# Half rows of the w2 gradient stored from ScalarE's DMA queue in place of GpSimd's

## The chip, the cores and the metric

The kernel runs on one core of a Trainium2 chip. The metric is the device time of one execution in microseconds (us). A core has TensorE (PE in the profile, its weight loads PEld), VectorE (DVE), ScalarE (ACT), GpSimd (POOL) and SyncE (SP); the last issues transfers only. Each engine takes its instructions in the order in which the built program holds them. Transfers between the chip's DRAM and SBUF are issued by SyncE and GpSimd here, and, in the changed kernel, by ScalarE as well.

## The reference, cut to what matters

The reference is a block of two halves and its gradients: a spectral mixing layer (a 2-D FFT, a product with complex weights w_r + i w_i, the inverse FFT) and an MLP, each behind a layer norm with adaptive scale and shift from a conditioning vector.

```python
def _B_ref(x, w1, b1, w2, b2):            # S=2048, D=1024, F=3584
    y = _layernorm(x, axis=-1)
    h = _gelu(jnp.einsum('bsd,df->bsf', y, w1) + b1)
    return jnp.einsum('bsf,fd->bsd', h, w2) + b2
mod = (_silu(c) @ w_mod).reshape(c.shape[0], 6, 1, -1)      # sa, ca, ga, sb, cb, gb
h = _layernorm(x, axis=-1) * (1 + ca) + sa
x = x + ga * _A_ref(h, A_w_r, A_w_i)      # spectral half
h = _layernorm(x, axis=-1) * (1 + cb) + sb
x = x + gb * _B_ref(h, B_w1, B_b1, B_w2, B_b2)
_out, _vjp = jax.vjp(_f, A_x, A_w_r, A_w_i, B_w1, B_b1, B_w2, B_b2, c, w_mod)
return (_out0, *_vjp(grad_out))
```

All inputs and outputs are bfloat16. The output that the change touches is the gradient of w2 (out_6, 3584 x 1024): h transposed times gb * grad_out, a sum over the 2048 tokens.

## The kernel before, in words

The work is a sequence of stages, all written for one core. Forward: modulation rows, spectral half, MLP. Backward: first the MLP's gradient towards its input (pg_pass, by four token blocks), then the backward spectral half (spectral_core with fwd False). The gradients of w2 and w1 are large matrix products that wait for nobody; they are cut into pieces (the generator `pieces`, L1226) and handed to TensorE between the steps of the backward spectral half, as filling (`fill`, L1277).

**The w2 gradient.** It has 28 blocks `fc` of 128 rows, each in two halves `h` of 512 columns. One half (gw2_product, L1088) is 16 matmuls of 128 x 128 x 512 (gw2_mm, L1075) into one of four PSUM buffers (`ps_f`, "gw2acc"), each with a transposed slice of the hidden activations as its weights. These slices, 128 x 2048 of d_hh, come by transposing loads from SyncE (hh_load, L1228) into a few buffers, two blocks ahead. gw2_out (L1078) copies the PSUM buffer to SBUF (L1082), on whatever engine `nc.any` picks when the program is built: a scheduler with a model of each engine's time places every instruction and breaks ties by it. For fc below 8 the rows go to five buffers and are stored whole (L1086). From fc 8 on, two rows `gwo` of two halves serve by turns, and each half is stored by itself (L1084) from GpSimd's queue: 40 stores of 128 x 512 elements, 128 KB each. A copy into a half must wait until the store that last read this half has landed.

**The backward spectral half** around it, by line:

- Eight pairs n = 0 to 7 (`pair`, L495). A pair is 16 matmuls on TensorE (pcs, L505), four copies on ScalarE (cs01b, L650), then a chain on VectorE (L173): Pt from cs01b, products with the weights ws (qa, qb), the sums R, and the gradient of the spectral weights in pf or empf. SyncE stores that gradient (L551) and loads the next values of pf and of ws (L493, L490); GpSimd does the mirrored rows with indirect transfers (L552, L491). Four halves of the w2 gradient are filled in behind each pair (beside_bwd, L1302).
- In between, single steps of another gradient, that of w_mod (gmod_ring, L981): SyncE loads a piece of w_mod into one of three buffers in otl (L986, 256 KB, and L989 for a new row), VectorE reduces it (L997) and writes the outer product (L999), GpSimd stores it (L1000).
- s_inv (L556) turns R into V: per quarter eight products "pv" (L565) of four matmuls, each emptied by a copy (L647, also by `nc.any`), on two PSUM buffers. Two quarters follow the sixth pair, two the eighth.
- Then four groups of "po" products (L630) whose copies go to VectorE and ScalarE (L635, L637), and the chain of consume_bwd (L1184) on VectorE. The rest of the w2 gradient, and then the w1 gradient (gw1acc, L1266, stored by L1271 from GpSimd's queue), fills TensorE until the end. Its operands are the loads n3n (L1251) and, transposed, gzh (L1217).

**Semaphores.** Every transfer reports its landing to a semaphore. The framework gives the transfers of the hardware queues (SyncE's, and ScalarE's where there are any) eight of them by turns, and the software queue of GpSimd eight others; a transfer is issued only when the one that used its semaphore before has landed.

Of the kernel before, what the change touches and what calls it, by code (L numbers as in the profile page):

```python
# [17 lines left out]
P = 128  # L18
# [17 lines left out]
def kernel(  # L36
# [24 lines left out]
    nc = tc.nc  # L61
# [870 lines left out]
    for g in range(7):  # L932
        wtile = reg.tile([P, 4, D], BF16, name=f"w1T_{g}", tag=W1T[g])
        for k in range(4):
            fc = g * 4 + k
# [142 lines left out]
    def gw2_out(acc, fc, h):  # L1078
        row = gwo5[fc % 5] if fc < 8 else gwo[:, fc % 2]
        half = slice(h * KH, (h + 1) * KH)  # L1080
        with tc.high_priority():
            nc.any.tensor_copy(out=row[:, half], in_=acc[:])  # L1082
        if fc >= 8:
            nc.gpsimd.dma_start(out=out_6[fc * P:(fc + 1) * P, half], in_=row[:, half])  # L1084
        elif h == 1:
            nc.gpsimd.dma_start(out=out_6[fc * P:(fc + 1) * P, :], in_=row)  # L1086

    def gw2_product(fc, h):  # L1088
        acc = ps_f("gw2acc")
        for t in range(NT):  # L1090
            gw2_mm(acc, fc, h, t)
        gw2_out(acc, fc, h)
# [133 lines left out]
    def pieces():  # L1226
# [18 lines left out]
        for fc, h, acc in last:  # L1245
            gw2_out(acc, fc, h)
# [120 lines left out]
```

## Time and profile before

| what | us |
|---|---|
| median of three runs (lowest, highest) | 1463.76 (1459.10, 1466.73) |
| the profiled execution: time | 1459.13 |
| its span, first to last instruction | 1457.3 |
| TensorE busy (6835 matmuls) | 1396.5 |
| VectorE busy | 1058.4 |
| ScalarE busy | 752.2 |
| GpSimd busy | 366.1 |
| the 40 stores of L1084 on GpSimd, first and last start | 1057.5, 1239.3 |
| one such issue on GpSimd, median | 0.552 |
| one copy of L1082 on ScalarE, median | 0.585 |
| TensorE busy in the 205 us from 1040 to 1245 | 198.52 |

Times inside an execution count from the span's first instruction. "A <- B" in a view of waits reads: A stood idle until B had ended. A line "start, us, engine, line, operation, tiles, xcount [idle before <- releaser]" is one of a timeline. The granted TensorE clock of the profiled execution was 0.992 of full speed on average. The difference of 1.8 us between time and span lies outside the first and last instruction.

### The profile page before, as it was taken

How to read it: one execution, taken by the hardware profiler on the slowest of the kernel's cores; microseconds unless marked ns; L12 is line 12 of the kernel's file. 1: busy time of each engine (PE TensorE's matmuls, PEld its weight loads, DVE VectorE, ACT ScalarE, POOL GpSimd, SP SyncE). 2: the span in 40 equal slices, each digit the busy share in tenths (PEclk: the TensorE clock that was granted, in tenths of full speed). 3: DMA queues.
4: the chain of work that ended last, by engine and by line, in shares of the span. 5: the costliest groups of instructions: out<-in, count | busy, mean ns of one | idle time of the engine just before them, and what ended most of it. 6: DMA issues, size and time to landing. Idle time of an engine off the chain costs nothing. (4 is left out here: it accounts for less than half of the span.)

```text
span 1457.3 us, 18411 instructions
## 1 busy us (share of the span) xinstructions
PE 1396.5 (96%) x6835; PEld 649.0 (45%) x6835; DVE 1058.4 (73%) x1483; ACT 752.2 (52%) x1065; POOL 366.1 (25%) x441
## 2 busy tenths in 40 slices
PE   5889999999999999999999999999999999999997
PEld 2434545444444444444444444344444445444443
DVE  5884786898799787887520889898467678898650
ACT  4675555857887766665305574342622434344211
POOL 6520451211112122122211011021245441222432
PEclk8999999999999999999999999999999999999999
DMA  9962473899887877697998275297699987766991
GB/s 333 286 214 70 142 235 115 270 255 337 257 203 278 259 250 233 201 264 241 277 297 245 74 271 185 107 270 176 181 217 254 254 233 213 194 191 180 297 279 65
DMA packets 358367, 324.28 MB, mean 223 GB/s; under 512 B 209386, under 2 KB 301056, under 8 KB 358022
## 3 DMA queue, kind: packets, MB, share of 16 engines
q1 hardware_dynamic: 324166, 207.71, 52.7%
q0 software_dynamic: 34112, 115.41, 22.6%
q8 instruction: 53, 0.87, 0.2%
q14 instruction: 36, 0.29, 0.1%
HBM read 162.06 MB, written 111.20 MB: 188 GB/s over the span
## 5 line engine op out<-in xcount | busy, mean ns | idle before, releaser
L684 PE MATMUL pp<-gBoT,wt 128*128 128x512 bf16 x896 | 197.9, 380 | 4.5 <-DMA wt<-in_B_w_dram 2.6
L950 PE MATMUL pg<-w1T,gzr 128*128 128x512 bf16 x896 | 197.1, 381 | 0.2 <-ACT gn3b L961 0.2
L1266 PE MATMUL gw1acc<-gzh,n3n 128*128 128x512 bf16 x896 | 195.4, 379 | 1.3 <-DMA gzh<-d_gz 1.3
L684 PEld LDWEIGHTS <-wt 128*128 128x128 bf16 x896 | 87.7, 98 | 109.4 <-issue 4.2
L950 PEld LDWEIGHTS <-gzr 128*128 128x128 bf16 x896 | 87.3, 98 | 108.7 <-issue 6.6
L802 PEld LDWEIGHTS <-w 128*128 128x128 bf16 x896 | 87.3, 98 | 108.8 <-issue 4.7
L1266 PEld LDWEIGHTS <-n3n 128*128 128x128 bf16 x896 | 87.4, 98 | 106.1 <-issue 2.7
L802 PE MATMUL pz<-n3Tb,w 128*128 128x512 bf16 x448 | 99.2, 379 | 1.6 <-DVE w2sD L875 1.4
L802 PE MATMUL pz<-n3Ta,w 128*128 128x512 bf16 x448 | 98.7, 379 | 1.1 <-ACT gt L805 1.1
L1075 PE MATMUL gw2acc<-gB,hhsA 128*128 128x512 bf16 x448 | 98.5, 379 | 1.0 <-DMA hhsA<-d_hh 1.0
L853 PEld LDWEIGHTS <-hhA 128*128 128x128 bf16 x608 | 59.0, 98 | 71.7 <-issue 1.4
L805 ACT ACTIVATE gt<-pz,b_col 128x512 bf16<-128x512 f32 x112 | 72.5, 684 | 34.2 <-PE pz L802 32.8
L1270 ACT CAST gwo<-gw1acc 128x512 bf16<-128x512 f32 x50 | 29.1, 583 | 113.6 <-PE gw1acc L1266 99.0
L173 DVE TENSOR_TENSOR gt<-gt,gt 128x2048 bf16<-128x2048 bf16 x56 | 68.3, 1223 | 22.4 <-ACT gt L813 21.2
L1082 ACT CAST gwo<-gw2acc 128x512 bf16<-128x512 f32 x46 | 26.7, 583 | 109.9 <-PE gw2acc L1075 75.6
L811 ACT ACTIVATE gt<-gt 128x2048 bf16<-128x2048 bf16 x28 | 53.5, 1910 | 55.7 <-DVE gt L173 55.7
L173 DVE TENSOR_TENSOR ct<-ct 128x2048 bf16<-128x2048 bf16 x64 | 75.9, 1218 | 1.8 <-DMA d_n<-ct 1.1
L1075 PEld LDWEIGHTS <-hhsA 128*128 128x128 bf16 x448 | 43.6, 98 | 53.0 <-DMA hhsA<-d_hh 1.7
L997 DVE CUSTOM_DVE_ANT_0 otl<-otl 128x1024 bf16<-128x1024 bf16 x24 | 29.1, 1223 | 49.9 <-DMA otl<-in_w_mod_dram 44.2
L807 ACT ACTIVATE gt<-gt 128x2048 bf16<-128x2048 bf16 x28 | 53.4, 1908 | 5.4 <-DVE hhC L173 2.5
L813 ACT ACTIVATE gt<-gt 128x2048 bf16<-128x2048 bf16 x28 | 53.5, 1909 | 0.5
L1271 POOL DMA_DIRECT2D out_dram<-gwo x56 | 30.6, 548 | 85.6 <-ACT gwo L1270 53.4
(325 smaller groups left out, 2531.5 us busy)
## 6 DMA issues: line engine op xcount, KB each, us to landing
gzr<-d_gz SPq DMA_DIRECT2D x28, 512.0 KB
wblk<-in_w_mod_dram SPq DMA_DIRECT2D x12, 1024.0 KB
out_dram<-otl POOLq DMA_DIRECT2D x48, 256.0 KB
out_dram<-gwo POOLq DMA_DIRECT2D x96, 128.0 KB
d_ph<-pho POOLq DMA_DIRECT2D x21, 512.0 KB
d_hh<-hhA POOLq DMA_DIRECT2D x19, 512.0 KB
w2sD<-in_B_w_dram SPq DMA_DIRECT2D x14, 512.0 KB
hhC<-d_ph SPq DMA_DIRECT2D x14, 512.0 KB
```

Of the source, the lines that this page charges most:

```text
L173: return nc.vector.tensor_tensor(out=out, in0=a, in1=b, op=op)
L684: last_pe[0] = nc.tensor.matmul(pp[:], lhsT=wt[:, fg % 2, cch, k * P:(k + 1) * P], rhs=gBoT[j][:, cch, :], start=(cch == 0), stop=(cch == ...
L802: last_pe[0] = nc.tensor.matmul(pz[:], lhsT=w1s[g][:, cch, k * P:(k + 1) * P], rhs=n3T[:, cch, :], start=(cch == 0), stop=(cch == NDC - 1))
L805: nc.scalar.activation(out=zb[:, k, :], in_=pz[:], func=ACT.Identity, bias=b1_col[:, fc:fc + 1], scale=1.0)
L807: nc.scalar.activation(out=av, in_=zb, func=ACT.Square)
L811: nc.scalar.activation(out=sg, in_=bv, func=ACT.Sigmoid, scale=2.0 * GK)
L813: nc.scalar.activation(out=bv, in_=bv, func=ACT.Sigmoid, scale=-2.0 * GK)
L853: last_pe[0] = nc.tensor.matmul(pbs[i][:], lhsT=hh[:, k, i * P:(i + 1) * P], rhs=wp[:, k, :], start=False, stop=(g == 6 and k == 3))
L950: last_pg[0] = nc.tensor.matmul(pgs[i][:], lhsT=gzs[b, g][:, k, i * P:(i + 1) * P], rhs=w1Ts[g][:, k, h * KH:(h + 1) * KH], start=(g == 0 ...
L1075: nc.tensor.matmul(acc[:], lhsT=hh_of(fc)[:, t, :], rhs=gBs[t // 4][:, t % 4, h * KH:(h + 1) * KH], start=(t == 0), stop=(t == NT - 1))
L1266: nc.tensor.matmul(acc[:], lhsT=n3ns[t // 4][:, t % 4, cch * P:(cch + 1) * P], rhs=gz2[t // 8][:, t % 8, :], start=(t == 0), stop=(t == NT ...
L1271: nc.gpsimd.dma_start(out=out_4[cch * P:(cch + 1) * P, fg * 512:(fg + 1) * 512], in_=ob)
```

## The change

For fc of 8 and more, the copy out of PSUM is bound to ScalarE (it was `nc.any`), and the store of the half row is issued from ScalarE's own queue, inside the same block of high priority, in place of GpSimd's. For fc below 8 nothing changes.

```diff
         with tc.high_priority():
-            nc.any.tensor_copy(out=row[:, half], in_=acc[:])
-        if fc >= 8:
-            nc.gpsimd.dma_start(out=out_6[fc * P:(fc + 1) * P, half], in_=row[:, half])
-        elif h == 1:
+            (nc.any.tensor_copy if fc < 8 else nc.scalar.copy)(out=row[:, half], in_=acc[:])
+            if fc >= 8:
+                nc.scalar.dma_start(out=out_6[fc * P:(fc + 1) * P, half], in_=row[:, half])
+        if fc < 8 and h == 1:
             nc.gpsimd.dma_start(out=out_6[fc * P:(fc + 1) * P, :], in_=row)
```

In the built program the 40 stores leave GpSimd's order and stand in ScalarE's, each behind the copy that it stores; in six places the four pcs copies of a pair stand between the two, and among the last four stores another copy of L1082. SyncE's instructions keep their order. The two copies of L1082 that VectorE had are ScalarE's now. Since the scheduler places the rest by its model, some other instructions move as well, none of them before the first of these stores: two copies of L647 from ScalarE to VectorE, and the order of po, gw1acc and of VectorE's chain in the consumer stage.

## Prediction

> **What bounds the kernel now.** I read the page first (busy shares, slices), then the waits of TensorE in the stretch that the change touches, then the timelines of VectorE, ScalarE and SyncE there. The page:
>
> ```profile
> PE 1396.5 (96%) x6835; PEld 649.0 (45%) x6835; DVE 1058.4 (73%) x1483; ACT 752.2 (52%) x1065; POOL 366.1 (25%) x441
> PE   5889999999999999999999999999999999999997
> DMA  9962473899887877697998275297699987766991
> ```
>
> TensorE is busy 96% of the span, and from 1280 us on it never rests (168.98 of 169.00 us), so it sets the end: a gain can only come out of its idle time, and any new idle time of its own is added to the end. The moved stores lie between 1055 and 1244 us. TensorE's idle time from 1040 to 1250, by releaser (us in total, times, longest):
>
> ```profile
> PE pv L565 <- DVE R L173: 1.8, 1, 1.8
> PE gw2acc L1075 <- DMA otl<-d_hh: 1.3, 1, 1.3
> PE gw1acc L1266 <- DMA gzh<-d_gz: 1.3, 1, 1.3
> PE po L630 <- DVE ct L635: 1.1, 1, 1.1
> PE gw2acc L1075 <- DMA hhsA<-d_hh: 1.0, 1, 1.0
> ```
>
> None of these is a store or the GpSimd queue. The stores do hold ScalarE: the view of line 1082 puts 12.6 us of ScalarE's idle time, in 5 places, down to a row whose last store had not landed. TensorE does not feel it, because gw2acc has four PSUM buffers, and a product takes 3.45 us. So what the change removes is off the path: 40 issues of 0.55 us on POOL (22 us of 366), the 27.5 us that POOL waited for those copies, and ScalarE's 12.6 us. **I cost all that at nothing**; the cover is TensorE's own work, and POOL's indirect stores (L552) do not come sooner, since they start 0.8 us after L551 has landed (semaphore times: 1105.67, start 1106.50; 1122.24, start 1123.07).
>
> **What it adds, one: 40 issues and 40 waits on ScalarE.** No ScalarE issue is in the trace. The nearest rows are L551 on SyncE (0.34 to 0.39 us, 128 rows of 1 KB) and L1084 on POOL (0.55). I take 0.4: 16 us in all, in gaps of 2.87 us before each copy. Nothing. The waits matter more. In the built program the hardware queues share eight semaphores by turns, so each store also waits until the transfer that last used its semaphore, mostly one of SyncE's, has landed. I set each against the landing that the semaphore times of before give. Most have landed by then. The long ones: the second store of the third pair waits for L493 (landed 1098.24, copy done 1089.5), about 8.7 us; the store that stands behind the sixth pair's pcs copies waits for an L986 (1138.65), about 6.6 us; the last store of the sixth pair waits for the load of d_hh that SyncE issues at 1148.04 (landed 1154.92). Behind a waiting store stand ScalarE's next PSUM copies. For the first two these are gw2acc copies, with three more buffers free, and pcs copies (L650), 5 us late at most, for which VectorE waits only at Pt, at 1108.26 where the copies now end at about 1103.5. Free. Behind the third stand the V copies (L647), on two buffers: ScalarE would be back at 1154.9, and TensorE would lose about 8 us. The other way round, SyncE's transfers now wait for ScalarE's stores; the closest such pair is a store landing at about 1093 for an L551 that goes out at 1101.67, so this is free.
>
> **Two: the scheduler moves two V copies to VectorE.** `nc.any` picks an engine when the program is built; with ScalarE waiting it now picks VectorE for the first copy of V0 and of V1. In the changed program VectorE's order is:
>
> ```
> L173 pf1<-qb2 x2           (end of the sixth pair)
> L997, L999 (otl, gu)       [waits for L986]
> L997, L999 (otl, gu)       [waits for the next L986]
> L647 V0<-pv (first of 8)
> ```
>
> and TensorE's third pv product waits for that copy (two buffers). Before, these rows ran so:
>
> ```profile
> 1144.89 14.01 PE L565 MATMUL pv<-smi,R 128*128 128x512 bf16 x64
> ...
> 1146.01 0.59 ACT L647 CAST V<-pv 128x512 bf16<-128x512 f32 x1
> ...
> 1152.48 1.30 DVE L173 TENSOR_TENSOR pf<-qb 128x1026 bf16<-128x1026 bf16 x2
> 1155.63 1.23 DVE L997 CUSTOM_DVE_ANT_0 otl<-otl 128x1024 bf16<-128x1024 bf16 x1 [1.85 <-DMA otl<-in_w_mod_dram]
> ...
> 1158.66 1.23 DVE L997 CUSTOM_DVE_ANT_0 otl<-otl 128x1024 bf16<-128x1024 bf16 x1 [1.27 <-DMA otl<-in_w_mod_dram]
> ...
> 1159.93 0.49 DVE L999 TENSOR_SCALAR otl<-otl,u_rt 128x1024 bf16<-128x1024 bf16 x1
> ```
>
> The reader is to see that TensorE starts pv at 1144.89 and ScalarE empties the first one at 1146.01, while VectorE is a pair behind: it comes free of the second L999 only at 1160.42. The copy takes 0.68 (the two VectorE copies of line 1082), so it ends at 1161.1. TensorE can do two pv of 0.865 us (14.01/16, less the overlap) and stands from 1146.6 to 1161.1: **14.5 us**. ScalarE's own wait (until 1154.9) is inside it. The second L997 cannot come sooner, for its load goes out behind the stores of the pair just finished:
>
> ```profile
> 1153.21 0.95 SPq L551 DMA_DIRECT2D out_dram<-pf  x2
> 1154.25 0.40 SPq L986 DMA_DIRECT2D otl<-in_w_mod_dram  x1
> ```
>
> **Three: what later gives back.** TensorE's next stretch is 14.5 us late: pcs ends at 1174.9 in place of 1160.5, the copies at about 1176.4, and VectorE's next pair starts then instead of at 1169.29, 7.1 us late; the last pair starts about 7.8 us late, R is done at about 1200.8, the V1 copy's place on VectorE is reached at about 1204. TensorE comes there at 1204.3. So its wait of 1.78 us for R goes, and the second moved copy costs nothing: **minus 1.8**. ScalarE's store ahead of V1 waits for the load n3n (landed 1197.40, now some 7 us later), which ends about when TensorE arrives: nothing, up to 3 if the load is slow.
>
> **Four: the consumer stage.** The order of the second group of po products changes: TensorE's first gw1 product, which needs the load gzh (landed 1243.30 in the semaphore times), now stands ahead of four po groups that it used to run after. Before, it lost 1.1 + 1.3 + 0.2 there; now it would wait after 16 po matmuls (1.9 us from 1237.4), about 4.0: **plus 1.5**. The 2.0 us at 1274 (po for ScalarE's L635) I leave as they are, give or take 1.
>
> **Sum** against the profiled execution (1459.13 us, span 1457.3): 1459.1 + 14.5 - 1.8 + 1.5 = 1473.3. That execution is the fastest of before's to 0.03 us; the median of the three is 4.6 higher, and on it the sum would be 1478. I take 1475.
>
> [...] The DMA share from 1040 to 1205 is 0.89 to 1.01, and a 256 KB load that lands in 3.2 us at 1182.83 takes 4 to 6 us before. [...] No row here has three queues.
>
> **Rivals.**
> *ScalarE's wait alone.* If VectorE reaches the V0 copy by 1155, five us sooner, the d_hh load sets the wait: 8.0 - 1.8 + 1.5, 1467. Against: its place is behind two loads that SyncE issues late. 10%.
> *The loads get slower.* VectorE comes to V0 by turns: pf ends, SyncE stores it, loads otl, L997, next pair. Starts of Pt: 1072.56, 1091.54, 1108.26, 1125.24, 1143.93, then 1160.42; 17.6 a turn against 15.6 for TensorE's pair. Each turn holds a landing of 4 to 6 us. With ScalarE's stores as a third queue beside it, half as much again is 2 us, over five turns 10: 1484. Against: the bytes are the same, and POOL's queue gets emptier. 14%.
> *The loads get quicker* (not slower than before). If the turns shrink, V0's copy comes in time: 13.8 us over five turns, so from 2.8 us a turn on the stall is gone, and 1459 is left. Landing like the row at 1182.83 (3.2) gives only some 7 over the five, that is 1466; the rest would have to come out of SyncE's issues (a transposing load takes 3 to 5). 6%.
> My forecast has 70%, by itself 1468 to 1481 (unknown landings either way, the run's spread of 7.6).
>
> The range 1464 to 1486 takes in the first two rivals and leaves out the third and the tail above. About 0.5% (7.3 us) is what a measurement of this kernel can tell from no change: slower by more has most of the forecast, all of the second rival and half of the first, 84%; within it 14%; faster 2%.
>
> **What would show it.** TensorE's waits of the changed kernel should have a line pv L565 <- DVE V L647 of 13 to 16 us, and the line for R should be gone; the timeline should show a ScalarE without copies from about 1146 to 1155, just ahead of L647. The waits for rows whose store has not landed should nearly vanish from line 1082, and POOL should lose some 22 us busy, with no effect. If the pv wait is released by ACT instead, the first rival holds; if it is over 20, the second. I am wrong altogether if TensorE's idle time between 1145 and 1205 has not grown.

## The result, and the profile after

The changed kernel takes 1470.45 us (median of 15 runs, 1468.40 to 1478.50), the kernel before beside it 1464.09 (15 runs, 1458.38 to 1467.34): the ratio is 1.0051, 95% interval 1.0036 to 1.0066, so 7.5 us slower (5.3 to 9.7). The profiled execution of the changed kernel is one of its slower ones: 1477.03, span 1475.2. The profiled one of before was among its fastest. The two traces are thus 17.9 us apart, and only a part of that is the change; the parts below are therefore taken from the stages, and from several traces of each kernel.

The page of the changed kernel first (busy time, TensorE's 40 slices, the granted clock in tenths):

```profile
PE 1401.7 (95%) x6835; PEld 650.0 (44%) x6835; DVE 1058.1 (72%) x1482; ACT 752.8 (51%) x1066; POOL 348.8 (24%) x401
PE   5889999999999999999899999999999599999998
PEclk8999999999999999999999999999999799999999
```

GpSimd has 40 issues and 17.3 us less to do, the engines do the same work otherwise, and one slice, the 32nd (1143 to 1180 us), has fallen from 9 to 5. The clock falls in the same slice. TensorE's waits from 1040 to 1250 say by whom:

```profile
PE pv L565 <- DVE V L647: 16.5, 1, 16.5
PE gw2acc L1075 <- DMA hhsA<-d_hh: 1.7, 2, 0.9
PE gw2acc L1075 <- DMA otl<-d_hh: 0.3, 1, 0.3
```

One wait of 16.5 us has come, for the V copy on VectorE, and the line for R is gone. TensorE's timeline at that place (start, duration, what; in brackets the idle time ahead):

```profile
1148.05 1.89 PE L565 MATMUL pv<-smi,R 128*128 128x512 bf16 x8
1166.45 15.13 PE L565 MATMUL pv<-smi,R 128*128 128x512 bf16 x56 [16.52 <-DVE V L647]
```

Before, 64 of these matmuls took 14.01 us, so 56 should take some 12.3; here they take 15.13. VectorE ahead of it:

```profile
1158.62 1.30 DVE L173 TENSOR_TENSOR pf<-qb 128x1026 bf16<-128x1026 bf16 x2
1160.30 1.23 DVE L997 CUSTOM_DVE_ANT_0 otl<-otl 128x1024 bf16<-128x1024 bf16 x1 [0.37 <-DMA otl<-in_w_mod_dram]
...
1163.97 1.27 DVE L997 CUSTOM_DVE_ANT_0 otl<-otl 128x1024 bf16<-128x1024 bf16 x1 [1.91 <-DMA otl<-in_w_mod_dram]
...
1165.28 0.53 DVE L999 TENSOR_SCALAR otl<-otl,u_rt 128x1024 bf16<-128x1024 bf16 x1
1165.73 0.67 DVE L647 CAST V<-pv 128x512 bf16<-128x512 f32 x1
```

The copy stands behind two L997 and two L999, the second L997 behind a load. And ScalarE (ACTq rows are its store issues):

```profile
1151.81 0.34 ACTq L1084 DMA_DIRECT2D out_dram<-gwo  x1
1152.25 0.59 ACT L1082 CAST gwo<-gw2acc 128x512 bf16<-128x512 f32 x1 [3.05 <-DMA out_dram<-gwo]
1159.91 0.36 ACTq L1084 DMA_DIRECT2D out_dram<-gwo  x1
1160.31 0.59 ACT L647 CAST V<-pv 128x512 bf16<-128x512 f32 x1 [7.48 <-DMA hhsA<-d_hh]
1168.35 0.59 ACT L647 CAST V<-pv 128x512 bf16<-128x512 f32 x1 [7.45 <-PE pv L565]
1170.06 0.59 ACT L647 CAST V<-pv 128x512 bf16<-128x512 f32 x1 [1.12 <-PE pv L565]
1171.77 0.59 ACT L647 CAST V<-pv 128x512 bf16<-128x512 f32 x1 [1.12 <-PE pv L565]
1172.99 0.59 ACT L647 CAST V<-pv 128x512 bf16<-128x512 f32 x1 [0.64 <-PE pv L565]
1173.85 0.59 ACT L647 CAST V<-pv 128x512 bf16<-128x512 f32 x1 [0.28 <-PE pv L565]
```

Two things are to be seen. ScalarE's last store of the sixth pair waits until 1159.91 for a d_hh load, with the first V copy behind it; SyncE issues that load only at 1154.22, when the row that the store is to send has been ready since 1152.84. And after the stand the products come 1.71 us apart, twice the 0.865 of later ones: TensorE's matmuls run at half speed for a while (14 of them start 0.38 to 0.43 us apart, the later ones 0.216).

The end of the program has changed too. The last line of the kernel, L1362, in the view of that line; a GpSimd DRAIN follows its last transfer (count, then shortest, median and longest in ns, first and last start). Before:

```profile
L1362 POOLq DRAIN  x3: 46/103/6193, 1450.4 to 1457.1; - x3
```

After:

```profile
L1362 POOLq DRAIN  x3: 46/103/3197, 1471.2 to 1475.0; - x3
```

It takes 3.2 us in place of 6.2, and all engines wait for it at the end: it is over at 1474.4, and the others go on at 1474.6 (before: 1456.6 and 1456.7). TensorE's last matmul ends 7.8 us ahead of the end before, 4.8 after.

### The profile page after: what moved, and what is told of

Same layout as the page of the kernel before. It is cut to its first block, busy times and chain, and to the rows that moved or that the text cites. A ratio compares the mean times of both kernels' runs of the same rounds, so it can differ in the third digit from the quotient of the medians.

```text
span 1475.2 us, 18389 instructions
## 1 busy us (share of the span) xinstructions
PE 1401.7 (95%) x6835; PEld 650.0 (44%) x6835; DVE 1058.1 (72%) x1482; ACT 752.8 (51%) x1066; POOL 348.8 (24%) x401
## 5 line engine op out<-in xcount | busy, mean ns | idle before, releaser
L1082 ACT CAST gwo<-gw2acc 128x512 bf16<-128x512 f32 x48 | 27.9, 585 | 112.4 <-PE gw2acc L1075 69.0
L997 DVE CUSTOM_DVE_ANT_0 otl<-otl 128x1024 bf16<-128x1024 bf16 x24 | 29.2, 1226 | 49.0 <-DMA otl<-in_w_mod_dram 42.4
L647 ACT CAST V<-pv 128x512 bf16<-128x512 f32 x60 | 35.1, 587 | 34.8 <-PE pv L565 27.2
```

The costliest lines, as they stand in the source:

```text
L647: nc.any.tensor_copy(out=out, in_=in_)
```

## The experiments

The theories. **A**: the loss is a wait ahead of pv: ScalarE waits behind its stores on shared semaphores, and the two V copies that the scheduler therefore gives to VectorE stand behind L997 and L999. **B**: ScalarE's wait alone would cost as much. **C**: the third queue slows the loads. **D, E**: two readings of the gap between traces and medians. **F**: the fixing of the copies on ScalarE is what costs. **G to J**: GpSimd's last drain.

### 1. V copies fixed on ScalarE

```
-    ... act_copy, s_copy, act_copy, consume_bwd, ...   # third: nc.any
+    ... act_copy, s_copy, s_copy, consume_bwd, ...     # nc.scalar.copy
```

> The changed kernel with the V copies of the backward pass (L647) fixed on ScalarE, so that the scheduler cannot hand two of them to VectorE; the stores stay on ScalarE's queue. Theory A (the stand of TensorE comes from the V copy queued behind VectorE's L997 and L999): the wait of pv falls from 16.5 us to what ScalarE's own wait for the d_hh load leaves; in the trace of the changed kernel ScalarE is free at 1160.3 and TensorE's second pv ends at 1149.8, so about 10, released by ACT; time 1464 to 1468. Theory B (ScalarE's wait behind its stores is already the whole cost, VectorE only ends a little later): the wait stays above 13 and the time at 1470. Theory C (the third queue slows the loads through the whole stage): the time stays at 1470, whatever the wait.

Measured: ratio to before 1.0028 (1.0012 to 1.0044), 5.4 us below the changed kernel timed beside it (experiment 3). The wait of TensorE, and ScalarE's rows:

```profile
PE pv L565 <- ACT V L650: 11.0, 1, 11.0
```

```profile
1151.33 0.59 ACT L1082 CAST gwo<-gw2acc 128x512 bf16<-128x512 f32 x1 [1.91 <-DMA out_dram<-gwo]
1160.56 0.36 ACTq L1084 DMA_DIRECT2D out_dram<-gwo  x1
1160.96 1.07 ACT L650 CAST V<-pv 128x512 bf16<-128x512 f32 x2 [9.05 <-DMA hhsA<-d_hh]
```

(L650 is the helper that copies on ScalarE.) A holds, B falls: VectorE's place is worth 16.5 less 11.0. What is left is ScalarE's own wait, for the d_hh load at the same place. The median of 1472.31 lies above the 1464 to 1468 that were expected because all kernels timed beside it ran higher (before: 1467.53).

### 2. Also 8 of the 40 stores back on GpSimd

```
-    nc.scalar.dma_start(out=out_6[...])
+    (nc.gpsimd if fc in (18, 19, 22, 23) else nc.scalar).dma_start(out=out_6[...])
```

> The first experiment's kernel, and the 8 stores of rows 18, 19, 22 and 23, which stand on ScalarE ahead of the V copies of V0 and V1, issued from GpSimd as before; 32 stores stay on ScalarE. Theory A: no wait of pv over 2 us in the stage, TensorE's idle time from 1040 to 1250 as in the kernel before (about 7 us), time 1464 give or take 2. Theory C (third queue): 32 of 40 stores still use it, so most of the 6.4 us stay, 1468 or more.

Measured: 0.9992 (0.9978 to 1.0007), as before. TensorE at the same place and at the second V:

```profile
1150.08 13.98 PE L565 MATMUL pv<-smi,R 128*128 128x512 bf16 x63
...
1199.08 3.84 PE L565 MATMUL pv<-smB,R 128*128 128x512 bf16 x10 [3.26 <-DVE R L173]
```

No stand ahead of the first V; the wait for R is back. Two of A's numbers missed: that wait is over 2 us, and TensorE's idle time from 1030 to 1260 is 14.1 us in place of about 7, 4.7 of them ahead of one product for its d_hh load. 32 of 40 stores still use ScalarE's queue, and the time is that of before. But GpSimd's last drain is 2.6 us shorter here than before (3.6 us), which hides a loss of that size in the stages: they may have lost 1.4 us, by the interval up to 3.6. So C falls as the whole cost, and a small one stays possible. TensorE's waits for d_hh loads speak against it: 0.3 to 6.7 us in the seven traces with 32 or more of these stores on ScalarE's queue, 0.2 to 6.1 in the five without. In a build that was not run, with these 8 stores on GpSimd but without the fixing of the V copies, the V copies of this stage are on ScalarE as before: it is the waiting stores that move them.

### 3. The changed kernel again

No edit.

> The changed kernel, unaltered, for a second profile. Theory D (the sum on the profiled executions, 17.9 us apart, is larger than the 6.4 us of the medians because the first profile of before is among its fastest executions and that of the changed kernel among its slowest): the wait of pv is again 13 to 17 us, TensorE's matmuls behind it are slow again (more than 2 us lost over 56 matmuls), and the span is anywhere from 1466 to 1477. Rival E (the wait itself varies from execution to execution, and is mostly shorter): the wait is 5 to 10 us.

Measured: 1477.68 (6 runs), ratio 1.0065 (1.0043 to 1.0087); the profiled execution has a span of 1471.7.

```profile
1162.28 14.19 PE L565 MATMUL pv<-smi,R 128*128 128x512 bf16 x55 [16.56 <-DVE V L647]
```

The stand is the same to 0.04 us and is followed by slow matmuls again (9 of them). E falls, for these two executions: the stand does not vary; what differs between them is mostly the time at which the stage begins (first pv at 1148.05 and 1143.83).

### 4. The kernel before again

No edit.

> The kernel before, unaltered, for a second profile. Theory D: the time lies at 1462 to 1467, and TensorE's idle time or its granted clock somewhere outside the changed stage accounts for the 3 to 8 us over the first profile. Rival E: the time is where it is because of TensorE's waits within the changed stage, from 1040 to 1250, which in the changed kernel lie under the stand of pv.

Measured: span 1463.9, 6.6 us above the first profile. By stages: 2.8 until the first pv, 0.5 in the first V, 1.5 in the second, 1.5 in the consumer stage. The second V:

```profile
1197.43 13.12 PE L565 MATMUL pv<-smB,R 128*128 128x512 bf16 x59 [3.44 <-DVE R L173]
```

Both theories have a part: the wait for R, which the changed kernel does not have, is 3.4 here and was 1.8 in the profile that the prediction was made from.

### 5. Only the fixing of the copies

```
-    nc.any.tensor_copy(out=row[:, half], in_=acc[:])
+    (nc.any.tensor_copy if fc < 8 else nc.scalar.copy)(out=row[:, half], in_=acc[:])
     (stores on GpSimd, as before)
```

> The kernel before with only the other half of the change: the PSUM copies of rows 8 to 27 fixed on ScalarE, every store still on the GpSimd queue. It moves two copies of the consumer stage from VectorE to ScalarE and nothing else. Theory A (the loss is in ScalarE's waits behind its stores and in the V copies that they push to VectorE): no pv wait over 4 us, the time that of the kernel before (ratio 0.998 to 1.002). Rival F (fixing the copies on ScalarE costs in the consumer stage): 2 us or more slower, with TensorE waiting at po or gw1acc. Theory G (GpSimd's last drain is longer the more transfers its queue has carried): the drain at the end stays at 6.2 us, as all 441 of its issues are there.

Measured: 1.0007 (0.9991 to 1.0024); no difference from before. The interval alone would still admit the 2 us of F (1.0014), but TensorE does not wait longer in the consumer stage: 3.5 us at po and 0.7 at gw1acc, against 3.1 and 1.3 in the first trace of before. F falls. The drain at the end is 6.2 us. The wait for R is 3.25 us here, and the matmuls behind it are slow:

```profile
1192.89 14.57 PE L565 MATMUL pv<-smB,R 128*128 128x512 bf16 x59 [3.25 <-DVE R L173]
```

Compare the row of experiment 4: the same 59 recorded matmuls took 13.12.

### 6. Only the queue

```
-    (nc.any.tensor_copy if fc < 8 else nc.scalar.copy)(out=row[:, half], in_=acc[:])
+    nc.any.tensor_copy(out=row[:, half], in_=acc[:])
     (stores on ScalarE, as after)
```

> The changed kernel with the copies left to the scheduler (nc.any), the stores on ScalarE's queue. Theory A: as the changed kernel, a pv wait of 15 to 18 us released by VectorE, matmuls slow for 2 to 3 us behind it, ratio 1.004 to 1.008. Rival F: if the fixing costs anything, this one is faster than the changed kernel by it, 2 us or more. Theory G: the last drain is 3.2 us, as with the changed kernel.

Measured: 1.0047 (1.0027 to 1.0067), drain 3.2 us.

```profile
1159.55 13.77 PE L565 MATMUL pv<-smi,R 128*128 128x512 bf16 x55 [15.13 <-DVE V L647]
```

The queue alone brings the stand and the loss. The slow matmuls behind it cost 1.5 us, less than the 2 to 3 that were expected.

### 7. The w2 gradient as before, 40 stores of the w1 gradient on ScalarE

```
-    nc.any.tensor_copy(out=ob, in_=acc[:])
-    nc.gpsimd.dma_start(out=out_4[...], in_=ob)
+    if fg >= 2: nc.scalar.copy(out=ob, in_=acc[:]); nc.scalar.dma_start(out=out_4[...], in_=ob)
+    else:       (as before)
```

> The kernel before, with its w2 gradient stores untouched, and 40 of the 56 stores of the w1 gradient (those of the third column group on) issued from ScalarE behind its copies. It leaves the same 401 issues on GpSimd as the changed kernel, by other stores. Theory G (the last drain goes with the number of transfers that GpSimd's queue has carried): 3.2 us in place of 6.2, and the span behind TensorE's last matmul 4.8 in place of 7.8; time 3 us below before (ratio 0.998), unless ScalarE's waits behind these stores hold TensorE at gw1acc. Rival H (the drain was shorter because the moved stores were those of the changed stage, or by the time that passed since): the drain stays at 6.2.

Measured: 0.9959 (0.9935 to 0.9982), 1459.11 against 1464.29: faster than both kernels. TensorE's last matmul ends 3.2 us before the end, but not for the reason given:

```profile
L1365 POOLq DRAIN  x3: 46/103/3504, 1422.8 to 1451.9; - x3
```

The long drain (3.5 us) begins at 1422.8, where GpSimd's last store now is, and ends some 23 us before TensorE does. It is hidden, not only shorter. The end is 4.6 us shorter by it, of the 6.0 us (2.6 to 9.5) that the timed runs gained; what the rest is was not looked into.

### 8. Both sets of stores on ScalarE

Experiment 2's kernel with experiment 7's edit.

> The second experiment's kernel (V copies on ScalarE, 32 of the w2 gradient stores on ScalarE's queue, 8 ahead of the V copies on GpSimd) and the 40 stores of the w1 gradient of the seventh experiment on ScalarE too: 369 issues are left on GpSimd. Theory G: the last drain is under 1.5 us (6.2 less 72 times 0.075 is 0.8), the time 3 to 5 us below before (ratio 0.997). Rival H: the drain is as in the second experiment, 3.6. Theory C (a third queue slows the loads): the ratio stays at 0.999 or above.

Measured: 0.9986 (0.9967 to 1.0006). The drain takes 9.0 us with the fewest issues of all (it is hidden as in 7), so G is wrong: its length does not go with the number of issues. C's bound of 0.999 lies inside the interval, so this run does not speak on C. That it is no faster than 7 is not explained; the two intervals overlap.

### 9. Experiment 1 with one store of the forty on GpSimd

```
-    nc.scalar.dma_start(out=out_6[...])
+    (nc.gpsimd if (fc, h) == (19, 1) else nc.scalar).dma_start(out=out_6[...])
```

> The first experiment's kernel (V copies on ScalarE, stores on ScalarE's queue) with one store of the forty issued from GpSimd: the last one of the sixth pair, which in the built program shares its semaphore with the d_hh load of that stage and on which ScalarE waited until 1160.5 in the first experiment's trace. Every other store keeps its place and its semaphore. Theory A (that one wait holds the V copies): ScalarE is back some 9 us sooner, the pv wait falls from 11.0 to 3 or less, no slow matmuls behind it, the time falls from 1.0028 of before to 0.999 to 1.001. Rival B2 (any store there makes ScalarE late, the next one takes over the wait): the pv wait stays above 6 and the ratio above 1.0015.

Measured: 1.0009 (0.999 to 1.0028).

```profile
1151.68 1.89 PE L565 MATMUL pv<-smi,R 128*128 128x512 bf16 x8
1157.43 14.80 PE L565 MATMUL pv<-smi,R 128*128 128x512 bf16 x55 [3.86 <-ACT V L650]
```

```profile
1155.87 0.34 ACTq L1084 DMA_DIRECT2D out_dram<-gwo  x1
1156.30 0.58 ACT L1082 CAST gwo<-gw2acc 128x512 bf16<-128x512 f32 x1 [3.58 <-DMA out_dram<-gwo]
1156.78 1.08 ACT L650 CAST V<-pv 128x512 bf16<-128x512 f32 x2
```

One store takes the wait from 11.0 to 3.9 us. That is A's mechanism, somewhat short of its number: the next store ahead of V now waits 3.6 us for another of ScalarE's own stores, and 12 matmuls behind the stand are slow, which A had excluded. The time alone would not show it, as its interval overlaps that of experiment 1. The stores ahead of this place keep their semaphores; each later one has another than in experiment 1, which the expectation excluded.

### 10. The kernel before, the last 8 stores of the w1 gradient on SyncE

```
-    nc.gpsimd.dma_start(out=out_4[...], in_=ob)
+    (nc.gpsimd if fg < 6 else nc.sync).dma_start(out=out_4[...], in_=ob)
```

> The kernel before, with the last 8 of the 56 stores of the w1 gradient issued from SyncE, which has nothing left to issue there, in place of GpSimd. Theory I (GpSimd's last drain takes 3 to 9 us from its last transfer on, whatever it is, and sets the end only because GpSimd issues the last store): GpSimd's drain starts some 27 us before the end and is over before TensorE's last matmul; 3.2 us remain from that matmul to the end in place of 7.8; ratio 0.996 to 0.998. Rival J (the end waits for the drain's work wherever it starts, or SyncE's stores are slower to land): 5 us or more remain, ratio 0.999 or above.

Measured: 0.9965 (0.995 to 0.998), 1461.55 against 1466.69.

```profile
L1362 POOLq DRAIN  x3: 46/103/5618, 1437.5 to 1459.3; - x3
```

The drain is 5.6 us, starts at 1437.5 and ends at 1443.1, ahead of TensorE's last matmul (1456.2); 3.4 us are left behind that. I holds: only the queue of the last eight stores was changed, and with it the place of GpSimd's last transfer; 5.1 us went (2.9 to 7.3), and 4.4 of them are seen in the trace at the end.

## Why the prediction was right, and where its terms were off

The main step held as it was put: the waiting stores on ScalarE, the V copies given to VectorE, their place behind L997 and L999, a stand of TensorE in front of the third pv, R's wait gone. The size was less good than the time: the terms add up to 14.2 us, and 7.5 were measured. The forecast of 1475 is only 4.6 above the measured median because the sum stands on before's profiled run, 5.0 below before's median of 15 runs, and that is luck; on the median of three the prediction itself has 1478.

Here are TensorE's stages in three traces of each kind, in us; the kernel with only the fixed copies (experiment 5) stands for before, the one with only the queue (6) for after. Each is from the first matmul of the named product to the end of the last, as the trace models it.

| stage | before, 4, 5 | mean | after, 3, 6 | mean | difference | predicted |
|---|---|---|---|---|---|---|
| first V | 14.0, 14.5, 15.1 | 14.5 | 33.5, 32.6, 30.8 | 32.3 | +17.8 | +14.5 |
| second V | 15.9, 17.4, 18.6 | 17.3 | 14.1, 13.8, 13.8 | 13.9 | -3.4 | -1.8 |
| consumer stage (po) | 112.6, 114.1, 113.9 | 113.5 | 112.6, 114.2, 114.6 | 113.8 | +0.3 | +1.5 |
| last matmul to end | 7.8, 7.8, 7.8 | 7.8 | 4.8, 4.8, 4.8 | 4.8 | -3.0 | 0 |

- **The removed stores cost nothing**: right in the stage (in experiments 5 and 6 no wait of TensorE is put down to a store or to GpSimd), and GpSimd's busy time fell by 22.5 us (366.1, 374.1 and 373.6 in the traces of before, 4 and 5; 348.8, 346.8 and 350.8 after, 3 and 6) where 22 was predicted. Wrong at the end: "I cost all that at nothing" left out that GpSimd's drain sets the end of the program. It fell by 3.0.
- **The waits on ScalarE's queue**: the early ones are free, as predicted; TensorE's idle time from 1040 to 1145 is 2.0 us, for d_hh loads, against 2.3 before. The two long ones came as ScalarE's idle time of 8.1 and 7.2 us, where 8.7 and 6.6 were predicted, and the waits for rows whose last store had not landed fell from 12.6 to 3.1 us. The store ahead of V waited for the d_hh load, as named, until 1159.9 (predicted 1154.9; 3.2 of the 5.0 us are the later start of the stage), and by itself costs 11.0 us where the first rival had 8.0 (experiment 1).
- **The stand**: 14.5 predicted, 16.5, 16.6 and 15.1 measured. VectorE's second L999 ended 17.8, 17.8 and 16.4 us after the first pv started, against 15.5, 15.7 and 17.0 in the traces of before, 4 and 5. That is 1.3 later in the mean, no more than the spread within three traces. The four turns of VectorE from the second to the sixth pair take 73.0 to 77.1 us in the seven traces with 32 or more of these stores on ScalarE's queue, and 71.1 to 74.1 in the five with none: some 2.5 us more in the mean. If that is the third queue and not ScalarE's waits, what the second rival feared is worth 0.6 us a turn and some 1 us at the stand. The rival's 2 us a turn ("half as much again") and 10 in all were the author's estimate, which no run shows.
- **The clock**, which no step of the prediction had: behind the stands of 16.5, 16.6, 15.1 and 11.0 us came 14, 9, 7 and 12 matmuls at 0.38 to 0.43 us in place of 0.216: 1.5 to 2.9 us in all. In the changed kernel's profile the granted clock of the records is 0.5 from 1155.26 to 1172.33, and 1.0 on both sides of that; TensorE stands until 1166.45, and its matmuls are 0.216 us apart again from 1172.35 on. The stretches at 0.5 in the profiles of before and after last 3.41, 6.83 or 17.07 us, apart from one at the very end of each. The traces do not tell how long a wait it takes: one of 3.44 us left the matmuls at full speed (experiment 4), one of 3.25 did not (5). In the changed kernel's profile even a wait of 2.2 us, up to 918.4, was followed by slow matmuls: TensorE was busy for 1.31 us of the 3.41 up to 919.74, and for the next 3.41 the granted clock was 0.50.
- **What comes back at the second V**: the mechanism is right, the size was read from the mildest execution. The wait for R is 1.8 us in the first profile, 3.4 and 3.2 in 4 and 5, and in 5 it is followed by 7 slow matmuls.
- **The consumer stage**: the predicted 1.5 came where it was placed. The waits of gw1acc for gzh and of po for VectorE are 3.9, 4.0 and 3.0 us, against 2.4, 2.6 and 1.2. But the wait of po for ScalarE's L635, which the prediction left as it was, went from 2.0, 3.3 and 3.0 to 0.3 in each. Slow matmuls behind the other waits (granted clock 0.5 for 3.4 us in experiment 3, 6.8 in 6, 3.4 in 5) bring the stage to +0.3.
- **A misread row**: the DMA share from 1160 to 1205 is 0.87, below the range of 0.89 to 1.01 that the prediction gives; nothing in the sum rests on it.

The differences sum to 11.7 us. The timed runs put the loss at 7.5 (5.3 to 9.7), and at 6.9 and 9.5 in experiments 6 and 3. Spans of like traces differ by some 6.5 us, a standard deviation of about 3.3, so the difference of two means of three is good to 2.7 or so; whether the remaining 2 to 5 us are chance stays open. The terms that the prediction lacked or had too small pull both ways: a longer stand with its slow matmuls adds 3.3, and the shorter drain, the larger give-back and the consumer stage take away 5.8.

## What to carry to other kernels

Here stores put behind copies on ScalarE's queue brought that queue's waits into the engine (idle times of 8.1, 7.2 and 7.5 us in the changed kernel's profile). Before such a move, list from the built program, for each such store, what it waits for and what stands behind it; here one of forty, sharing a semaphore with a load that SyncE issued after the row was ready, made 7.1 of the 11.0 us that TensorE stood for ScalarE (experiments 1 and 9). When a library picks engines, compare the built order on every engine, not the diff. When pricing a stand of TensorE, look in the trace for a slow restart and add it (1.5 to 2.9 us behind the stands of 3.9 to 16.6 us here), and look at the program's last microseconds too: here GpSimd's drain set the end, and the last eight stores on SyncE's queue, with nothing left to issue but one small store, brought the time to 0.9965 (experiment 10).

## What the runs showed that was not expected

- GpSimd's last DRAIN takes 3.2 to 9.0 us, the same to 0.01 us in the two traces of before and of the changed kernel (6.193 and 6.197; 3.197 and 3.193), but not in the order of its number of issues: 6.2 us with 441 instructions on GpSimd, 5.6 with 433, 3.6 with 409, 3.2 and 3.5 with 401, 9.0 with 369. What sets it is open; it was not tried further.
- TensorE's slow restart costs 1.5 to 2.9 us. Of the waits of pv, it came after the five of 3.9 to 16.6 us and after those of 3.25 and 3.26 us (experiments 5 and 2), and not after the 3.44 us of experiment 4 or the 1.8 us of the first profile of before.
- A store issued from ScalarE costs 0.34 us of its queue (0.55 on GpSimd). The trace of the changed kernel tells the landing of only 4 of the 40: 2.0, 4.6, 5.4 and 5.6 us after the issue.
